# The first block of the hidden gradients read by transposing loads, and two more pairs of weight-gradient stores issued by ScalarE, in a long-convolution plus gated-MLP backward kernel

## The chip, the cores and the metric

The kernel runs on one core of one Trainium2 chip. The metric is device time in microseconds (us), the median of several executions. The engines of the core are TensorE (PE in the profile, with its weight loads shown as PEld), VectorE (DVE), ScalarE (ACT), GpSimd (POOL) and SyncE (SP), which in this kernel issues most of the DMAs. Each engine works through its own queue of instructions in order, and semaphores hold the queues in step.

## The reference, cut to what matters

The program computes a forward pass and all its gradients, in bf16, with S = 2048 rows, D = 512 and F = 1376:

```
xn  = layernorm(q)                              # 2048 x 512
ksh = sum_t shift_k[:, 3-t] * k shifted by t    # four taps
kv  = ksh * v
y   = causal convolution of kv with ssm_k (length 2048, by FFT) + kv * ssm_D
h   = (xn @ Wg) * (xn @ Wu)                     # 2048 x 1376
out = q + xn * y + h @ Wd
outputs: out, and from grad_out the gradients of
         q, k, v, shift_k, ssm_k, ssm_D, Wg, Wu, Wd
```

The part that matters here is the gated MLP. With go = grad_out, its backward pass makes dh = go @ Wd^T, du = dh * (xn @ Wg) and dg = dh * (xn @ Wu), and then the three weight gradients: dWd = h^T @ go, dWg = xn^T @ dg and dWu = xn^T @ du. These three sum over the 2048 rows, so h, dg and du are needed with rows on the partitions, while the forward stage makes them with F on the partitions. Something has to turn them.

## The kernel before

**Tiling.** The 2048 rows lie as 16 rows on each of 128 partitions (R = 16). The first stage works in NCH = 8 chunks of 256 rows. F is cut into NFB = 11 blocks, numbered 0 to 10, ten of 128 and a last one of 96.

**Stage one.** `ffn1(ch)` (L497) makes, for each chunk, a tile `hd` that holds h, dg and du for all eleven blocks, F on the partitions, and stores chunks 0 to 6 to a DRAM scratch `HDD` (L536). Chunk 7 stays in the core. `yb(ch)` (L539) multiplies `hd` by the weights to get the output and the input gradient of the MLP: matmuls into `py` (L548) and `px` (L555); a VectorE addition (L550) adds the loaded rows of q (`xb`, L543) to `py`, and the result `bx` goes to the scratch `BX`. Between these pieces a generator `side` advances the convolution; its last products are cast into `GO` and stored to the scratch `GD` (L619).

**Where the stages meet.** When stage one has no more `ffn1` to do (tag "wa", L897), the pools of two weights are closed, and in their room the core loads `goC` (L902) and `xnC` (L903), go and xn for all rows, 2 MB each. `open_c` (L862) then opens the pools "n" (the turned tiles `nath` and `natd`) and "b" (`g1` and `hb`), and loads blocks 0 and 1 of `HDD` into two `hb` tiles and the first two `g1` tiles out of `GD`.

**How a block is turned.** There are two ways. In the first, block fb is loaded as it lies into `hb` (`load_hb`, L793), and `hid_t(fb, t)` (L846) for t = 0, 1, 2 does 16 TensorE transposes each into a PSUM tile `pt` (L859), which ScalarE copies into `nath` (h) or `natd` (dg and du). Block 0 is turned so between the pieces of `yb(7)`. In the second way, used for the blocks in `TURNED` (6 to 10), `load_t` (L804) issues a transposing DMA (L817) that lands chunks 0 to 6 already turned in a tile `natT`; `last_t` (L824) turns only chunk 7, with 6 TensorE transposes (L829) and one ScalarE copy into `nat7`. `behind` names a DMA that the transposing load of a block must be issued behind.

**The weight gradients.** `dw()` (L1050) goes through the blocks. `down_grad(fb)` makes dWd of the block (`pd`, 16 matmuls, L1038), a cast `od`, and a store. Then come 64 matmuls into `pu` (L1068) for dWg and dWu of the block, and a cast into `og` (L1075). `og` holds two blocks, so after each odd block two stores (L1079, one for dWg and one for dWu) take it to DRAM; there is one `og` buffer. These stores are issued by SP, for blocks 9 and 10 by ScalarE. Halfway through `pu` of block fb, `last_t(fb + 1)` is called if block fb + 1 is a turned one.

**What runs beside it.** Other generators are interleaved with `dw()`: the last transform of y and its gradient (`inv_y`: `pq`, L932, with casts `yC` and `dd`), the gradient of shift_k (`dsk_gram`: `pk`, L1091; its 2 KB result `dskb` is stored at L1107 in pieces of 8 bytes), the gradient of ssm_k (`inv_dk`: `po`, L1003, with casts into `o5t`), and the final elementwise work on VectorE, whose results `o`, `e` and `dk` are stored by SP at L1183. All casts and copies that the helper `act` makes appear under its line, L235.

**What sets the order.** A tile framework puts the instructions in order from priorities, and `issue_after` pins one DMA behind another. The PSUM pool of `pt`, `pu`, `pq`, `po` and `pk` has three buffers, taken in turn. Each DMA issued by SP or ScalarE takes, in program order, the next of eight completion counters. A DMA waits on its issuing engine until the transfer that used its counter before, usually the eighth before it, has landed. While it waits, everything behind it on that engine's queue waits too.

Of the kernel before, what the change touches and what calls it, by code (L numbers as in the profile page):

```python
# [8 lines left out]
BF = mybir.dt.bfloat16  # L9
# [9 lines left out]
D = 512  # L19
F = 1376  # L20
R = 16
P = 128
NC4 = 4
FBLK = [(i * 128, min(128, F - i * 128)) for i in range((F + 127) // 128)]
NFB = len(FBLK)
NCH = 8
# [164 lines left out]
def kernel(  # L191
# [24 lines left out]
    nc = tc.nc  # L216
# [29 lines left out]
    HDD = dram.tile([P, NFB, NCH - 1, 3, 256], BF, name="HDD")  # L246
# [409 lines left out]
    first = ExitStack()  # L656
# [122 lines left out]
    CP = {}  # L779
    nats = {}  # L780
    pend = []

    def load_g1(sg, r0):
        t = CP["b"].tile([P, 2, 4, D], BF, name="g1")
        LG["g"] = nc.sync.dma_start(t[:], GD[sg, :, :, r0:r0 + 4, :])
        return t

    LG = {}

    def load_hb(fb):  # L790
        f0, fw = FBLK[fb]
        t = CP["b"].tile([P, NCH - 1, 3, 256], BF, name="hb")
        nc.sync.dma_start(t[:fw], HDD[:fw, fb])  # L793
        hbs[fb] = t

    hbs = {}

    TURNED = range(NFB - 5, NFB)

    def behind(fb):  # L800
        first = {NFB - 5: lambda: DKS["kb", R - 2], NFB - 3: lambda: LG["gk"], NFB - 2: lambda: LG["bb"], NFB - 1: lambda: LG["og"]}.get(fb)
        return tc.issue_after(first().ins) if first else ExitStack()

    def load_t(fb):  # L804

        f0, fw = FBLK[fb]
        if fb == SPLIT:
            parts = ((0, 5, "n", dict(tag="natd", bufs=2)), (5, NCH - 1, "n", dict(tag="nath")))
        elif fw < P:
            parts = ((0, NCH - 1, "n", dict(tag="natd", bufs=2)),)  # L810
        else:
            parts = ((0, NCH - 1, "b", dict(tag="hb")),)
        nats[fb, 0] = {}
        for a, e, pool, kw in parts:
            t = CP[pool].tile([P, e - a, 3, 2, fw], BF, name="natT", **kw)
            with behind(fb) as _, tc.high_priority(offset=SOON):
                nc.sync.dma_start_transpose(out=t[:].rearrange("s c t h f -> s (c t h) f"),  # L817
                                            in_=HDD[:fw, fb, a:e].rearrange("p c t s -> p (c t s)"))
            for c in range(a, e):
                nats[fb, 0][c] = t[:, c - a]  # L820

    SPLIT = NFB - 3
# [23 lines left out]
    def hid_t(fb, t):  # L846
        if fb in TURNED:
            return
        f0, fw = FBLK[fb]
        hb = hbs.pop(fb) if t == 2 else hbs[fb]  # L850
        if t == 0:
            nats[fb, 0] = CP["n"].tile([P, R, P], BF, name="nath")
        elif t == 1:
            nats[fb, 1] = CP["n"].tile([P, 2, R, P], BF, name="natd", bufs=2)
        dst = nats[fb, 0] if t == 0 else nats[fb, 1][:, t - 1]
        pt = P2("pt", [P, R, P], BF)
        for r in range(R):
            hs = hb[:fw, r // 2, t] if r < R - 2 else hds[1][:fw, fb, t]
            nc.tensor.transpose(pt[:, r, :fw], hs[:, (r % 2) * 128:(r % 2) * 128 + 128], ident[:fw, :fw])  # L859
        act(dst[:, :, :fw], pt[:, :, :fw])  # L860

    def open_c():  # L862
        for _ in side:
            pass
        gpool["es"].close()
        CP["n"] = ctx.enter_context(tc.tile_pool(name="c1n", bufs=1, reuse_waits="tile"))
        CP["b"] = ctx.enter_context(tc.tile_pool(name="c1b", bufs=2, reuse_waits="tile"))
        load_hb(0)
        load_hb(1)
        pend.extend((load_g1(0, 0), load_g1(1, 0)))  # L870

    def main():
        for ch in range(NCH):
            it = ffn1(ch)
            for n, set_here in enumerate(it):
                if ch == 0:
                    tables(n)
                yield set_here
                if n == 1 and 0 < ch < NCH - 1:
                    load_xt(ch + 1)  # L880
                if n == (5 if ch == 1 else 1) and 0 < ch < NCH - 1:
                    while len(WTS) < 2:
                        next(side)
                    yield from yb(ch - 1)
        yield "wa"
        yield from yb(NCH - 2)
        open_c()
        for n, tag in enumerate(yb(NCH - 1)):
            yield tag
            if 2 < n < 6:  # L890
                hid_t(0, n - 3)

    mainit = main()
    acc = -4 * pace[0]
# [1 line left out]
    for tag in mainit:  # L896
        if tag == "wa":  # L897
            wa_es.close()
            c1 = ctx.enter_context(tc.tile_pool(name="c1", bufs=1, reuse_waits="tile"))
            xnC = c1.tile([P, R, D], BF, name="xnC")  # L900
            goC = c1.tile([P, R, D], BF, name="goC")
            nc.sync.dma_start(goC[:], go_n)  # L902
            nc.sync.dma_start(xnC[:], XN[:])  # L903
        if pace[0] is None:

            if tag and tag != "wa":
                next(side, None)
            continue
        if tag != "half":
            acc += pace[0]  # L910
        while acc >= 1 and pace[0]:
            acc -= 1
            next(side, None)
# [28 lines left out]
    DKS = {}  # L942
# [44 lines left out]
        return lambda c, i: ts[c, i // 2][:, i % 2]  # L987

    def inv_dk():
        o5t = c2.tile([P, NC4, P, R], BF, name="o5t", tag="o5k")  # L990
        o5 = out_5.rearrange("(c q) s -> c q s", q=P)
        for rq in range(4):
            gk = gks.pop(0)
            if rq == 2:
                sides[2][1] = 2
            if rq == 0:
                gk_last = load_gk_last()
            for b in range(2):
                po = P2("po", [P, 2, 4, P])
                for h in range(2):  # L1000
                    for i in range(4):
                        for c in range(2):
                            nc.tensor.matmul(po[:, h, i, :], lhsT=(gk_last(c, i) if rq == 3 else gk[:, c, i])[:, cs(2 * b + h)], rhs=TB.IW[:, c, :],  # L1003
                                             start=(c == 0), stop=(c == 1))
                act(o5t[:, 2 * b:2 * b + 2, :, 4 * rq:4 * rq + 4], po[:].rearrange("q h r s -> q h s r"))
                if b == 1 and rq < 2:
                    gks.append(load_gk(2) if rq == 0 else None)
                if rq == 3:
                    for c in (2 * b, 2 * b + 1):
                        nc.scalar.dma_start(o5[c], o5t[:, c].rearrange("q s r -> q (s r)"))  # L1010
                yield
            if rq == 0:
                yield from put_dD(o5t)
# [35 lines left out]

    def dw():  # L1050
        og = None
        load_hb(2)
        for fb, (f0, fw) in enumerate(FBLK):
            last = fb + 1 == NFB
            if not last:
                down_grad(fb)
                yield
                hid_t(fb + 1, 0)
                hid_t(fb + 1, 1)
                yield  # L1060
                yield
            pu = P2("pu", [P, NC4, 2, P])
            if fb % 2 == 0:
                og = c2b.tile([P, 2, NC4, P], BF, name="og1", tag="dd") if last else c2.tile([P, 2, NC4, 2 * P], BF, name="og")
            q0 = (fb % 2) * P
            for c in range(NC4):
                for r in range(R):
                    nc.tensor.matmul(pu[:, c, :, :fw], lhsT=xnC[:, r, cs(c)], rhs=nat_d(fb, r),  # L1068
                                     start=(r == 0), stop=(r == R - 1))
                if c == 1:  # L1070
                    yield
                    if fb + 1 in TURNED:
                        last_t(fb + 1)
                    yield
            act(og[:, :, :, q0:q0 + fw].rearrange("p t c f -> p c t f"), pu[:, :, :, :fw])  # L1075
            if fb % 2 == 1 or last:
                a = f0 - q0
                for t, o in enumerate((out_7, out_8)):
                    LG["og"] = (nc.scalar if fb + 2 >= NFB else nc.sync).dma_start(o[:, a:f0 + fw].rearrange("(c p) f -> p c f", p=128), og[:, t, :, :q0 + fw])  # L1079
            yield  # L1080
            if last:
                down_grad(fb)
                yield
# [76 lines left out]
    KH = []  # L1160

    def load_kh():
        khC = c2.tile([P, R + 3, D], BF, name="khC", tag="o5k")
        nc.gpsimd.memset(khC[0:1, 0:3, :], 0.0)
        with tc.issue_after(LG["g"].ins):
            nc.sync.dma_start(khC[:, 3:3 + R, :], k_n)
            nc.sync.dma_start(khC[1:113, 0:3, :], k_n[0:112, R - 3:R, :])
            nc.sync.dma_start(khC[113:128, 0:3, :], k_n[112:127, R - 3:R, :])
        KH.append(khC)
# [72 lines left out]
```

## Time and profile before

| what | value |
|---|---|
| time, median of three runs | 477.08 us (475.93 to 478.26) |
| time of the profiled execution | 475.32 us |
| its span | 473.5 us |
| granted TensorE clock | 1.00 |
| PE busy | 464.8 us (98%) |
| DVE busy | 339.4 us (72%) |
| ACT busy | 304.6 us (64%) |
| POOL busy | 13.9 us (3%) |
| DMA | 139.86 MB, mean 295 GB/s |

Times in the profile count from the start of the span. The profiled execution lies 1.82 us above its own span and 1.76 us below the median of the runs. A row of a timeline gives the start, the duration, the engine, the line, the operation and its operands, and in brackets how long the engine was idle before it and what released it. "SPq" and "ACTq" are DMAs issued by SyncE and by ScalarE; the duration there is that of the issue, not of the transfer.

### The profile page before, as it was taken

What the parts mean: (1) busy time and instruction counts of PE and PEld (TensorE: products, weight loads), DVE (VectorE), ACT (ScalarE), POOL (GpSimd) and SP (SyncE); (2) the same over time, 40 slices, a digit from 0 to 9 for tenths busy, and PEclk for the clock granted to TensorE, in tenths of its full rate; (3) what the DMA queues carried; (4) which work ended last, traced back from release to release, by engine and by line L of the source; (5) the groups of instructions that cost most, each with busy time, mean ns of one, the idle gap of its engine ahead of it and who ended that gap; (6) DMA issues with size and microseconds to landing.
All of it is one profiled execution on the core that took longest, in us unless ns stands there. A gap on an engine that the chain in (4) does not pass through costs nothing.

```text
span 473.5 us, 10352 instructions
## 1 busy us (share of the span) xinstructions
PE 464.8 (98%) x4263; PEld 310.5 (66%) x4263; DVE 339.4 (72%) x609; ACT 304.6 (64%) x357; POOL 13.9 (3%) x30
## 2 busy tenths in 40 slices
PE   7999999999999999999999999999999999999997
PEld 6877754547638548447537753467776777878887
DVE  7889989989356566777857878113137899799695
ACT  4957777759567678879779975275865664233242
POOL 8000000000000000000000000110000000000000
PEclk9999999999999999999999999999999999999999
DMA  8999999999997958968978369998999999999996
GB/s 264 377 368 383 307 304 328 316 326 321 322 289 262 263 187 256 303 190 263 284 234 277 133 199 367 358 360 289 350 350 365 372 317 333 304 269 313 203 312 199
DMA packets 116917, 139.86 MB, mean 295 GB/s; under 512 B 44776, under 2 KB 90249, under 8 KB 115463
## 3 DMA queue, kind: packets, MB, share of 16 engines
q1 hardware_dynamic: 112598, 135.03, 90.5%
q10 hardware_dynamic: 4272, 4.18, 2.7%
q8 instruction: 33, 0.54, 0.5%
q14 instruction: 14, 0.11, 0.1%
HBM read 65.70 MB, written 63.41 MB: 273 GB/s over the span
## 4 chain that ended last, share of the span: by engine, by line
PE 85%; DMA 8%; DVE 5%; ACT 1%; issue 1%; ACTq 0%
PE pu L1068 16%; PE px L555 16%; PE pgu L512 13%; PE py L548 8%; PE pd L1038 7%; PE pdh L518 6%; PE pt L859 3%; PE pq L932 3%; PE ps L584 3%; PE pg L613 3%; DMA ssk<-in_A_ssm_k_dram 3%; PE pf L370 3%; DMA x_b<-in_A_q_dram 2%; PE pk L1091 2%; PE po L1003 2%; DMA XN<-x_b 1%
## 5 line engine op out<-in xcount | busy, mean ns | idle before, releaser
L555 PE MATMUL px<-WT,hd 128*128 128x512 bf16 (+1 forms) x352 | 81.0, 380 | 0.0
L1068 PEld LDWEIGHTS <-xnC 128*128 128x128 bf16 x704 | 67.1, 98 | 8.2 <-issue 0.4
L555 PEld LDWEIGHTS <-hd 128*128 128x128 bf16 (+1 forms) x352 | 32.8, 98 | 44.4 <-issue 7.7
L235 ACT CAST gu<-pgu 128x1024 bf16<-128x1024 f32 (+1 forms) x48 | 45.4, 945 | 17.3 <-PE pgu L512 16.8
L235 ACT CAST GO<-pg 128x1024 bf16<-128x1024 f32 x48 | 46.2, 1015 | 13.8 <-issue 7.2
L235 ACT CAST SP<-ps 128x1024 bf16<-128x1024 f32 x47 | 45.6, 1026 | 13.7 <-PE ps L584 11.8
L600 DVE TENSOR_TENSOR T<-SP 128x2048 bf16<-128x2048 bf16 x24 | 29.3, 1222 | 34.8 <-ACT SP L235 34.7
L512 PE MATMUL pgu<-xt,Wu 128*128 128x256 bf16 (+1 forms) x352 | 53.1, 273 | 0.7 <-DVE kn L238 0.6
L512 PE MATMUL pgu<-xt,Wg 128*128 128x256 bf16 (+1 forms) x352 | 52.8, 273 | 0.2 <-DMA Wg<-in_B_w_gate_dram 0.2
L518 PE MATMUL pdh<-gt,WdT 128*128 128x256 bf16 (+1 forms) x352 | 46.9, 272 | 0.1
L235 ACT CAST fst<-pf 128x1024 bf16<-128x1024 f32 x44 | 42.7, 1031 | 5.4 <-ACT fst L235 2.1
L1068 PE MATMUL pu<-natd,xnC 128*128 128x256 bf16 x384 | 43.9, 273 | 0.0
L512 PEld LDWEIGHTS <-Wu 128*128 128x128 bf16 (+1 forms) x352 | 33.0, 100 | 15.1 <-issue 10.0
L548 PE MATMUL py<-Wd,hd 128*128 128x512 bf16 (+1 forms) x176 | 41.4, 380 | 0.0
L518 PEld LDWEIGHTS <-WdT 128*128 128x128 bf16 (+1 forms) x352 | 34.9, 100 | 4.8 <-issue 0.2
L512 PEld LDWEIGHTS <-Wg 128*128 128x128 bf16 (+1 forms) x352 | 34.8, 100 | 4.1 <-DMA Wg<-in_B_w_gate_dram 0.5
L1068 PE MATMUL pu<-natT,xnC 128*128 128x256 bf16 (+1 forms) x280 | 32.3, 267 | 0.0
L532 DVE TENSOR_TENSOR hd<-gu 128x512 bf16<-128x512 bf16 (+1 forms) x48 | 19.1, 397 | 17.3 <-ACT gu L235 17.3
L533 DVE TENSOR_TENSOR hd<-gu,dh 128x1024 bf16<-128x1024 bf16 (+1 forms) x48 | 30.8, 642 | 0.8
L235 ACT CAST og<-pu 128x1024 bf16<-128x1024 f32 (+1 forms) x11 | 10.9, 993 | 30.8 <-PE pu L1068 21.4
L548 PEld LDWEIGHTS <-hd 128*128 128x128 bf16 (+1 forms) x176 | 16.5, 98 | 20.8 <-issue 3.1
L600 DVE TENSOR_TENSOR U<-SP 128x2048 bf16<-128x2048 bf16 x24 | 29.2, 1218 | 0.0
(178 smaller groups left out, 685.9 us busy)
## 6 DMA issues: line engine op xcount, KB each, us to landing
HDD<-hd SPq DMA_DIRECT2D x35, 384.0 KB, 4.6
FD<-fst SPq DMA_DIRECT2D x24, 512.0 KB, 5.0
X<-FD SPq DMA_DIRECT2D x24, 512.0 KB, 5.4
GD<-GO SPq DMA_DIRECT2D x24, 512.0 KB, 3.7
g<-GD SPq DMA_DIRECT2D x11, 1024.0 KB, 8.1
hb<-HDD SPq DMA_DIRECT2D x6, 1344.0 KB, 8.4
bb<-BX SPq DMA_DIRECT2D x8, 512.0 KB, 6.8
BX<-bx SPq DMA_DIRECT2D x7, 512.0 KB, 3.9
```

The source lines that it names most:

```text
L235: nc.scalar.copy(o, i)
L370: nc.tensor.matmul(pf[:, c, :], lhsT=TB.W1[:, c, :], rhs=src[:, i, :], start=True, stop=not point)
L512: nc.tensor.matmul(pgu[:w, i, t, :], lhsT=W[:, c, f0:f0 + w], rhs=xt[:, :, c, :], start=(c == 0), stop=(c == NC4 - 1))
L518: nc.tensor.matmul(pdh[:w, i, :], lhsT=WdT[:, c, f0:f0 + w], rhs=gt[:, :, c, :], start=(c == 0), stop=(c == NC4 - 1))
L532: nc.vector.tensor_tensor(hd[:fw, fb0:fb0 + n, 0, :], gu[:fw, :n, 0, :], gu[:fw, :n, 1, :], op=ALU.mult)
L533: nc.vector.tensor_tensor(hd[:fw, fb0:fb0 + n, 1:3, :], gu[:fw, :n], dh[:fw, :n].unsqueeze(2).to_broadcast((fw, n, 2, 256)), op=ALU.mult)
L548: nc.tensor.matmul(py[:], lhsT=hd[:fw, fb, 0, ss], rhs=Wd[:fw, fb, :], start=(fb == 0), stop=(fb == NFB - 1))
L555: nc.tensor.matmul(px[:], lhsT=hd[:fw, fb, t, ss], rhs=W[:fw, fb, :], start=(t == 1 and fb == 0), stop=(t == 2 and fb == NFB - 1))
L584: nc.tensor.matmul(ps[32 * q:32 * q + 32, a, :], lhsT=TB.EF[64 * a:64 * a + 64, 4 * g + q, ri].rearrange("p k j -> p (k j)"), rhs=X[64 * a ...
L600: tt(W[:].rearrange("p c a d -> p c (a d)"), A[:, i:i + 1].rearrange("p c a d -> p c (a d)").to_broadcast((P, 2, 2 * D)), B[:].rearrange(" ...
L1038: nc.tensor.matmul(pd[:fw, :], lhsT=nat_h(fb, r), rhs=goC[:, r, :], start=(r == 0), stop=(r == R - 1))
L1068: nc.tensor.matmul(pu[:, c, :, :fw], lhsT=xnC[:, r, cs(c)], rhs=nat_d(fb, r), start=(r == 0), stop=(r == R - 1))
```

## The change

Block 0 joins the turned blocks. Its transposing load is cut in two: chunks 0 to 4 go into a tile of the pool "n", which is now opened at tag "wa", and SP issues this load ahead of `goC` and `xnC`; chunks 5 and 6 go into a tile that shares its room with `o5t` and `khC` (a new pool "o") and are loaded in `open_c` behind the first `g1`. The plain load of block 0 is gone, and so are its 48 transposes in `yb(7)`; `last_t(0)` runs at the start of `dw()`. `natd` tiles now alternate between two pools instead of taking two buffers of one. The load of block 2 into `hb` comes directly behind that of block 1 and the second `g1`. The stores of `og` of blocks 3 and 7 go from SP to ScalarE. The transposing load of block 10 is pinned behind the load of `bb` instead of behind the stores of `og`.

```diff
-    TURNED = range(NFB - 5, NFB)
+    TURNED = (0, *range(NFB - 5, NFB))
...
-        first = {..., NFB - 1: lambda: LG["og"]}.get(fb)
+        first = {..., NFB - 1: lambda: LG["bb"]}.get(fb)
...
+    def natd(shape, name):
+        i = len(turn) % 2
+        turn.append(i)
+        return CP["nm"[i]].tile(shape, BF, name=name, tag=f"natd{i}")
...
-    def load_t(fb):
+    def load_t(fb, part=None):
         f0, fw = FBLK[fb]
-        if fb == SPLIT:
+        if part is not None:
+            parts = (((0, 5, None, {}),), ((5, NCH - 1, "o", dict(tag="o5k")),))[part]
+        elif fb == SPLIT:
...
-                nc.sync.dma_start_transpose(out=..., in_=...)
+                LG["t"] = nc.sync.dma_start_transpose(out=..., in_=...)
...
     def open_c():
...
-        CP["n"] = ctx.enter_context(tc.tile_pool(name="c1n", bufs=1, reuse_waits="tile"))
+        CP["m"] = ctx.enter_context(tc.tile_pool(name="c1m", bufs=1, reuse_waits="tile"))
         CP["b"] = ctx.enter_context(tc.tile_pool(name="c1b", bufs=2, reuse_waits="tile"))
-        load_hb(0)
+        CP["o"] = ctx.enter_context(tc.tile_pool(name="c1o", bufs=1, reuse_waits="tile"))
+        pend.append(load_g1(0, 0))
+        load_t(0, 1)
         load_hb(1)
-        pend.extend((load_g1(0, 0), load_g1(1, 0)))
+        pend.append(load_g1(1, 0))
...
         yield from yb(NCH - 2)
         open_c()
-        for n, tag in enumerate(yb(NCH - 1)):
-            yield tag
-            if 2 < n < 6:
-                hid_t(0, n - 3)
+        yield from yb(NCH - 1)
...
+            CP["n"] = ctx.enter_context(tc.tile_pool(name="c1n", bufs=1, reuse_waits="tile"))
+            load_t(0, 0)
             nc.sync.dma_start(goC[:], go_n)
             nc.sync.dma_start(xnC[:], XN[:])
...
     def dw():
         og = None
-        load_hb(2)
+        with tc.issue_after(LG["t"].ins):
+            load_hb(2)
+        last_t(0)
...
-                    LG["og"] = (nc.scalar if fb + 2 >= NFB else nc.sync).dma_start(...)
+                    LG["og"] = (nc.scalar if fb in (3, NFB - 4, NFB - 2, NFB - 1) else nc.sync).dma_start(...)
```

More of the change, by code (lines that the diff above doesn't have):

```diff
@@ L796 @@
     hbs = {}
-    TURNED = range(NFB - 5, NFB)
+    TURNED = (0, *range(NFB - 5, NFB))
     def behind(fb):
-        first = {NFB - 5: lambda: DKS["kb", R - 2], NFB - 3: lambda: LG["gk"], NFB - 2: lambda: LG["bb"], NFB - 1: lambda: LG["og"]}.get(fb)
+        first = {NFB - 5: lambda: DKS["kb", R - 2], NFB - 3: lambda: LG["gk"], NFB - 2: lambda: LG["bb"], NFB - 1: lambda: LG["bb"]}.get(fb)
         return tc.issue_after(first().ins) if first else ExitStack()
-    def load_t(fb):
+    turn = []
+    def natd(shape, name):
[3 more added lines that the diff above has]
+    def load_t(fb, part=None):
         f0, fw = FBLK[fb]
-        if fb == SPLIT:
-            parts = ((0, 5, "n", dict(tag="natd", bufs=2)), (5, NCH - 1, "n", dict(tag="nath")))
+        if part is not None:
+            parts = (((0, 5, None, {}),), ((5, NCH - 1, "o", dict(tag="o5k")),))[part]
+        elif fb == SPLIT:
+            parts = ((0, 5, None, {}), (5, NCH - 1, "n", dict(tag="nath")))
         elif fw < P:
-            parts = ((0, NCH - 1, "n", dict(tag="natd", bufs=2)),)
+            parts = ((0, NCH - 1, None, {}),)
         else:
             parts = ((0, NCH - 1, "b", dict(tag="hb")),)
-        nats[fb, 0] = {}
+        if not part:
+            nats[fb, 0] = {}
         for a, e, pool, kw in parts:
-            t = CP[pool].tile([P, e - a, 3, 2, fw], BF, name="natT", **kw)
+            shape = [P, e - a, 3, 2, fw]
+            t = CP[pool].tile(shape, BF, name="natT", **kw) if pool else natd(shape, "natT")
             with behind(fb) as _, tc.high_priority(offset=SOON):
-                nc.sync.dma_start_transpose(out=t[:].rearrange("s c t h f -> s (c t h) f"),
-                                            in_=HDD[:fw, fb, a:e].rearrange("p c t s -> p (c t s)"))
+                LG["t"] = nc.sync.dma_start_transpose(out=t[:].rearrange("s c t h f -> s (c t h) f"),
+                                                      in_=HDD[:fw, fb, a:e].rearrange("p c t s -> p (c t s)"))
             for c in range(a, e):
@@ L853, in hid_t @@
         elif t == 1:
-            nats[fb, 1] = CP["n"].tile([P, 2, R, P], BF, name="natd", bufs=2)
+            nats[fb, 1] = natd([P, 2, R, P], "natd")
         dst = nats[fb, 0] if t == 0 else nats[fb, 1][:, t - 1]
@@ L989, in inv_dk @@
     def inv_dk():
-        o5t = c2.tile([P, NC4, P, R], BF, name="o5t", tag="o5k")
+        o5t = CP["o"].tile([P, NC4, P, R], BF, name="o5t", tag="o5k")
         o5 = out_5.rearrange("(c q) s -> c q s", q=P)
@@ L1078, in dw @@
                 for t, o in enumerate((out_7, out_8)):
-                    LG["og"] = (nc.scalar if fb + 2 >= NFB else nc.sync).dma_start(o[:, a:f0 + fw].rearrange("(c p) f -> p c f", p=128), og[:, t, :, :q0 + fw])
+                    LG["og"] = (nc.scalar if fb in (3, NFB - 4, NFB - 2, NFB - 1) else nc.sync).dma_start(o[:, a:f0 + fw].rearrange("(c p) f -> p c f", p=128), og[:, t, :, :q0 + fw])
             yield
@@ L1162, in load_kh @@
     def load_kh():
-        khC = c2.tile([P, R + 3, D], BF, name="khC", tag="o5k")
+        khC = CP["o"].tile([P, R + 3, D], BF, name="khC", tag="o5k")
         nc.gpsimd.memset(khC[0:1, 0:3, :], 0.0)
```

## The prediction, made before the changed kernel had run

> **What bounds the kernel now.** I began with the page's head, its busy times and the shares of the chain that ended last.
>
> ```profile
> span 473.5 us, 10352 instructions
> ...
> PE 464.8 (98%) x4263; PEld 310.5 (66%) x4263; DVE 339.4 (72%) x609; ACT 304.6 (64%) x357; POOL 13.9 (3%) x30
> ...
> PE 85%; DMA 8%; DVE 5%; ACT 1%; issue 1%; ACTq 0%
> ```
>
> PE is busy for 98% of the span, so only two things move the time much: PE work added or removed, and stalls of PE. The change touches two places. For the first, where block 0 is turned, the chain that ended last, in order of time:
>
> ```profile
> 305.60 0.87 PE px L555 x4
> 306.47 0.89 PE pt L859 x16
> 307.36 1.51 PE px L555 x7
> 308.87 0.90 PE pt L859 x16
> 309.77 2.38 PE px L555 x11
> 312.15 0.90 PE pt L859 x16
> 313.04 3.45 PE pd L1038 x16
> ```
>
> The three batches of transposes stand between matmuls with no gap: what they cost is PE time on the path. For the second place, where block 7's `og` is stored, SP's timeline:
>
> ```profile
> 428.47 9.52 SPq L817 DMA_TRANSPOSE natT<-HDD  x1
> 438.08 0.53 SPq L1045 DMA_DIRECT2D out_dram<-od  x1
> 438.66 0.42 SPq L1107 DMA_DIRECT2D out_dram<-dskb  x1
> ...
> 442.38 0.97 SPq L1079 DMA_DIRECT2D out_dram<-og  x2
> 445.71 6.70 SPq L817 DMA_TRANSPOSE natT<-HDD  x1
> ```
>
> and ScalarE's, where the last three lines show what a ScalarE store does when the transfer that had its counter is still out:
>
> ```profile
> 435.65 1.01 ACT L235 CAST og<-pu 128x1024 bf16<-128x1024 f32 x1 [2.69 <-PE pu L1068]
> 436.55 1.02 ACT L235 CAST o5t<-po 128x1024 bf16<-128x1024 f32 x1
> ...
> 461.59 1.01 ACT L235 CAST og<-pu 128x1024 bf16<-128x1024 f32 x1 [2.19 <-PE pu L1068]
> 464.88 1.94 ACTq L1079 DMA_DIRECT2D out_dram<-og  x2
> 466.87 0.80 ACT L235 CAST og<-pu 128x768 bf16<-128x768 f32 x1 [4.27 <-PE pu L1068]
> ```
>
> Block 9's cast ends at 462.60, yet its stores issue at 464.88 and the next cast starts only behind them: ScalarE stood. Last, PE's row for the chunk-7 transposes of block 9, and a line of SP's waits:
>
> ```profile
> 444.18 0.50 PE L829 MATMUL pt<-ident,hd 128*128 128x128 bf16 x6
> ```
>
> ```profile
> SPq L817 <- DMA out_dram<-dskb: 2.3, 1, 2.3
> ```
>
> The `dskb` store, issued at 438.66, lands only at 445.66 (7.0 us for 2 KB in 8-byte pieces, behind block 9's transposing load); whoever has its counter next waits for it. Before, that was the transposing load of block 10 on SP, with no harm to PE.
>
> **The change part by part.** All sums are on the clock of the profiled execution (475.32 us, span 473.5), which lies 1.76 below the median of 477.08; I add that back at the end.
>
> *Transposes.* Removed from PE: 0.89 + 0.90 + 0.90 = 2.69 us. Added: six transposes for chunk 7, by the step between PE rows at 444.18 and 444.51, 0.33 us. Net −2.35. ScalarE loses three copies (1.86 each at 307.40, 309.81, 313.18) and gains one of 0.80; no PE instruction waited there, so nothing either way. Bounds: 0 if the same stretch becomes a stall, −2.35 if none does; I take −2.35, since the loads come in time:
>
> *Loads.* The plain load of block 0 (1.34 MB) goes; 0.98 MB and 0.39 MB of transposing loads come. The first stands on SP ahead of `goC`, `xnC`, a `GD` store and `xb`. Up to now the DMA engines are empty from 274 to 278 (share 0.00) and full from 282 to 294 (0.99, 382 GB/s). `xb`, issued at 290.74, landed at 295.4; in the changed kernel it must be in and the 0.69 us addition done before PE's second `py` of `yb(7)` at 303.06, which takes the same PSUM buffer. The load pushes it by 0.98 MB at 382 GB/s (2.6 us) or, if what counts is SP's issue time, by 6.2 us (7.65 for block 8's two parts less 1.39 for the smaller); a 0.5 MB `GD` store now ahead adds 1.4. So `xb` lands between 299.4 and 303.0: a stall of 0 to 0.6, and I take 0. The other first users have more room: the small part (chunks 5 and 6) lands about 307 and `pd` needs it near 312; `g1` about 311 against 314; block 1 about 314 against 315.7; block 2 about 320 against 330. Later transposing loads are far ahead: block 9's landed at 441.6 for PE at 448.9.
>
> *One tile fewer.* `nat7` of block 0 sits in one of the two `dd` buffers until `pu(0)` ends, so the second `dd` cast must wait for VectorE's two products of the first (until about 326.8 instead of 325.4). The next cast it could delay is `og` at 328.76: 0.
>
> *Stores of block 3.* They wait for a `g1` load and a part of `khC`, both landed by 375.4, while the cast of block 3 ends at 379.49. ScalarE pays two issues of about 0.45 us; ScalarE is 64% busy and no PE row waits for it there. 0; bounds 0 to 0.9.
>
> *Stores of block 7.* By the order of DMAs and the eight counters, the first must wait for the `od` store of SP 438.08 (landing 442.1), the second for `dskb` (445.66). Queued behind them on ScalarE: the cast `o5t` that ran at 436.55, then `od`, `o5t`, `nat7`. PE's six transposes for block 9 take the PSUM buffer which that first `o5t` cast must empty. So they can start at 445.66 + 0.45 (second issue) + 1.02 (cast) + about 0.1 = 447.2 instead of 444.18, a stall of 3.1 us. Both ends move together if SP's chain moves with PE: block 7's transposing load (398.05) waited 7.2 us for PE, and the `og` stores of 412.31 follow a cast driven by PE, so everything up to `dskb` should be 2.35 earlier, like PE itself. Bounds: 0 (no stand, or `dskb` in before 440.2 on the new clock) and 5.4 (SP's chain keeps its old times, 3.1 + 2.35). I take 3.1, nearest to the rows.
>
> *The tail.* Behind it nothing is gained back: PE follows on without idle. `og` of block 8 is cast when the late stores have landed; `pu` of block 9 has 1.07 us of room (cast end 452.18, `pu` 453.25), which a landing of 2.6 us, the median of ScalarE's `og` stores, leaves whole. VectorE's last `dk`, today 0.35 us in the way of the last `od` store, is earlier with SP, so −0.3.
>
> Sum: −2.35 + 3.1 − 0.3 = +0.45: 475.8 on the profiled clock, 477.5 against the median.
>
> [...]
>
> **The rivals.** *A: the cover holds.* ScalarE doesn't stand long enough to stop PE, because `dskb` lands early or the stores' counters are free. For it: only 2 KB are written, and PE has never yet waited for a ScalarE store. Against: the order of transfers gives exactly this counter, and ScalarE did stand at 462.60 to 464.88. It gives −2.35 to −2.65: 474.6. [...]
>
> *B: slower, SP's chain stays where it is.* One mechanism, at one place: `dskb` lands on the old clock. The chain ahead of it is 7.65 and 9.52 us of issue for transposing loads; if these are bound by the engines that move them (share 1.41 from 434 to 440) and not by PE's release, PE arrives 2.35 us early and waits 5.4. Price: −2.35 + 5.4 − 0.3 = +2.8, 479.8. It decides from a landing of `dskb` at about 445.3 on the new clock. The stores of ScalarE in the same engines could push it there too. Against: SP was released by PE at 398.05.
>
> *C: the front is late as well.* `xb` or `goC` comes after the issue of 6.2 us plus more traffic, PE loses about 1 us at 303: with the main case 478.5. For it: SP's slowest bound above is 0.6 already; against: 4 us of empty DMA engines ahead of it.
>
> **How the numbers follow.** Main case (gain eaten by the ScalarE stand, 476.7 to 478.5 with 0 to 1 for C): 0.53, with C in it. A: 0.22. B: 0.25. The bound that a measurement of this kernel can tell is 0.5%, 2.4 us: faster means below 474.7, slower above 479.5. A's 474.4 to 474.7 lies at or under the one and B's 479.9 at or over the other, so the chances are nearly the cases' own: faster 0.21, same 0.54, slower 0.25. Range: from A's lower end, 474.4, to B's with 0.4 for a late `xb`, 480.2. The main case's own range is 476.7 to 478.7.
>
> **What would show it.** In the changed profile: `px` of `yb(7)` in one piece with no `pt`, and `pd` of block 0 about 2.35 us earlier than 313.04 (else C, at the row of the second `py`); on ScalarE a gap between `og` of block 7 and its two stores, and the first `o5t` only behind the second; a PE idle of about 3 us ahead of the six transposes of block 9; the landing of `dskb` on the new clock, 443.3 for the main case, 445.3 or later for B, before 440.5 for A. The prediction is wrong if PE shows no idle there, if the idle is over 5, or if a new PE wait appears elsewhere, at `pu` of block 9 or `po`, for which no row of before gives a reason.

## The result, and the profile after

The changed kernel is slower: 480.62 us median of nine runs (478.24 to 482.92), against 476.69 us of the kernel before in as many (475.63 to 478.26). The ratio is 1.0084, with a 95% interval of 1.006 to 1.0109: 2.9 to 5.2 us more. (The ratios in this document leave out executions that took over 1.5% more than the fastest of their kernel, and so are not the quotient of the two medians beside them, which are over all executions.) The forecast was 477.5, in a range from 474.4 to 480.2, with 0.25 for slower by over 0.5%. The median lies 0.4 us above the range.

The profiled execution of the changed kernel took 480.96 us, with a span of 479.2, 5.7 more than the span of before. Its page begins:

```profile
span 479.2 us, 10219 instructions
...
PE 462.3 (96%) x4181; PEld 310.2 (65%) x4221; DVE 339.0 (71%) x609; ACT 299.9 (63%) x355; POOL 14.0 (3%) x30
...
PE 79%; DMA 12%; DVE 6%; issue 1%; ACT 1%; ACTq 0%; SPq 0%; DVEq 0%
```

PE's busy time is 2.5 us lower (this trace has 4181 matmuls for 4221 weight loads, so some matmul records are missing from it), and the span is longer. PE's share of the chain that ended last fell from 85% to 79%, and DMA's rose from 8% to 12%. The chain itself, in order of time:

```profile
305.97 1.30 PE px L555 x6
307.27 0.05 issue
307.32 3.41 PE px L555 x15
310.73 0.34 PE pt L840 x6
311.07 3.45 PE pd L1050 x16
...
365.83 15.41 DMA hb<-HDD
381.25 0.05 issue
381.30 1.96 PE pt L870 x32
...
439.46 5.52 DMA out_dram<-od
444.98 0.02 issue
445.00 0.02 ACTq L1093
...
446.27 1.02 ACT o5t L235
447.29 0.04 issue
447.33 0.80 PE pt L840 x6
448.13 5.89 PE pu L1082 x32
```

Three things are to be seen. The `px` matmuls run on with no transposes between them, and six transposes stand ahead of `pd`. At 365.83 a load is on the path that was not there before: block 5's plain load, which reaches PE at 381.25. And from 439.46 the chain leaves PE altogether: a store of `od`, ScalarE's two stores of `og`, the `o5t` cast, and only then PE's six transposes for block 9. Here are SP's and ScalarE's timelines of that place, and PE's row; SP's first row is block 7's load, the second block 9's.

```profile
396.73 10.31 SPq L828 DMA_TRANSPOSE natT<-HDD  x1
...
429.69 9.68 SPq L828 DMA_TRANSPOSE natT<-HDD  x1
439.46 0.52 SPq L1057 DMA_DIRECT2D out_dram<-od  x1
440.04 0.42 SPq L1121 DMA_DIRECT2D out_dram<-dskb  x1
...
444.80 7.95 SPq L828 DMA_TRANSPOSE natT<-HDD  x1
```

```profile
434.32 1.01 ACT L235 CAST og<-pu 128x1024 bf16<-128x1024 f32 x1 [2.69 <-PE pu L1082]
445.06 1.17 ACTq L1093 DMA_DIRECT2D out_dram<-og  x2
446.27 1.01 ACT L235 CAST o5t<-po 128x1024 bf16<-128x1024 f32 x1 [10.94 <-issue]
```

```profile
447.33 0.80 PE L840 MATMUL pt<-ident,hd 128*128 128x128 bf16 x6 [4.31 <-ACT o5t L235]
447.93 3.19 PE L1082 MATMUL pu<-natT,xnC 128*128 128x256 bf16 x14
```

ScalarE stood from 435.33, the end of block 7's cast, to 445.06, and PE was idle for 4.31 us. The counters can be read in this trace: its 322 DMAs of SP and ScalarE take eight semaphores in turn, 40 or 41 on each, and ScalarE's two stores here have those of `od` and `dskb`, which were full at 444.98 and 445.16; the stores issued at 445.06 and 445.49. And behind the idle PE's rows are longer for the same work: six transposes in 0.80 us, where the row of before says 0.50, and 14 `pu` matmuls in 3.19 where the others say 1.69. The windows of the changed kernel say why; the columns are the busy times of PE, PEld, DVE, ACT and POOL, the granted clock of PE, the DMA share and the GB/s:

```profile
443.00:447.00 4.00, 0.02 (x1) 0.00 (x0) 3.44 (x7) 0.73 (x1) 0.00 (x0) 0.89 0.83 196
...
448.00:450.00 2.00, 2.00 (x12) 1.40 (x10) 1.79 (x4) 1.39 (x2) 0.00 (x0) 0.50 0.98 177
450.00:452.00 2.00, 2.00 (x12) 1.34 (x10) 1.93 (x4) 0.00 (x0) 0.00 (x0) 0.50 1.24 247
452.00:454.00 2.00, 2.00 (x17) 1.63 (x16) 1.97 (x6) 0.00 (x0) 0.00 (x0) 0.77 1.24 258
```

The granted clock is a half from about 446 to 453. It was 1.00 in these windows before, and the mean over the span is 0.993 or 0.996 in all nine executions of the changed kernel.

From these rows the 5.7 us can be followed. PE's positions, changed less before: +0.38 at 271 us, before any changed instruction (the `pdh` rows at 271.38 and 271.00); −1.98 at `pd` of block 0 (310.90 and 312.88), so the turning gave 2.36; −1.32 at block 5's transposes (381.30 and 382.62), so 0.66 was lost at the late load; +3.15 at block 9's six transposes (447.33 and 444.18), so the stand took 4.47; +5.85 at the `po` matmuls behind block 8's `pu` (453.86 and 448.01), so the half clock took 2.70; then level to the end, where the tail gives 0.15 back.

### The profile page after: what moved, and what is told of

Read it like the earlier page. It is cut to its first block, busy times and chain, and to the rows that moved or that the text cites. A ratio compares the mean times of both kernels' runs of the same rounds, so it can differ in the third digit from the quotient of the medians.

```text
span 479.2 us, 10219 instructions
## 1 busy us (share of the span) xinstructions
PE 462.3 (96%) x4181; PEld 310.2 (65%) x4221; DVE 339.0 (71%) x609; ACT 299.9 (63%) x355; POOL 14.0 (3%) x30
## 4 chain that ended last, share of the span: by engine, by line
PE 79%; DMA 12%; DVE 6%; issue 1%; ACT 1%; ACTq 0%; SPq 0%; DVEq 0%
PE px L555 15%; PE pu L1082 14%; PE pgu L512 13%; PE py L548 7%; PE pd L1050 6%; PE pdh L518 6%; DMA hb<-HDD 3%; PE ps L584 3%; PE pf L370 3%; PE pg L613 3%; DMA ssk<-in_A_ssm_k_dram 2%; PE pq L944 2%; PE pt L870 2%; DMA x_b<-in_A_q_dram 2%; PE pk L1105 2%; PE po L1015 1%
## 5 line engine op out<-in xcount | busy, mean ns | idle before, releaser
L555 PE MATMUL px<-WT,hd 128*128 128x512 bf16 (+1 forms) x340 | 78.5, 379 | 1.6 <-issue 1.4
L1082 PEld LDWEIGHTS <-xnC 128*128 128x128 bf16 x704 | 68.4, 100 | 9.4 <-issue 0.4
L1082 PE MATMUL pu<-natT,xnC 128*128 128x256 bf16 (+1 forms) x336 | 41.4, 277 | 0.0
L548 PE MATMUL py<-Wd,hd 128*128 128x512 bf16 (+1 forms) x167 | 40.2, 379 | 0.8 <-issue 0.5
L1082 PE MATMUL pu<-natd,xnC 128*128 128x256 bf16 x320 | 36.6, 273 | 0.0
```

What stands on the lines that cost most here:

```text
L548: nc.tensor.matmul(py[:], lhsT=hd[:fw, fb, 0, ss], rhs=Wd[:fw, fb, :], start=(fb == 0), stop=(fb == NFB - 1))
L555: nc.tensor.matmul(px[:], lhsT=hd[:fw, fb, t, ss], rhs=W[:fw, fb, :], start=(t == 1 and fb == 0), stop=(t == 2 and fb == NFB - 1))
```

## The experiments

**The loads alone.** Block 0 turned by transposing loads as in the change; all stores and the pin of block 10's load as before.

```diff
-  (nc.scalar if fb in (3, NFB - 4, NFB - 2, NFB - 1) else nc.sync)
+  (nc.scalar if fb + 2 >= NFB else nc.sync)
-  NFB - 1: lambda: LG["bb"]
+  NFB - 1: lambda: LG["og"]
```

> The changed kernel's loads without its moves of stores: block 0 turned by transposing loads; all og stores and the pin of block 10's load as in the kernel before. Theory: first pd of block 0 about 2.35 us earlier than before, of which about 0.65 is lost at block 5's plain load, which lands at the same clock time as before; 1.7 us under the kernel before, 475.0. Rival (the transfers are shared out so that nothing is gained): the time of before within 0.5 us. Rival (nothing is late next): 2.35 under, 474.3.

Measured: 474.55 us against 476.18, ratio 0.997 (0.9946 to 0.9993). Its span is 472.4. `pd` of block 0 starts 39.53 us after the `pdh` row near 271, against 41.88 before: 2.35 gained, to the hundredth what was forecast for the turning. In this execution block 5's load was in time, as the second rival had it. So the loads are a small gain by themselves, and the whole loss belongs to the moved stores and the moved pin.

**Block 3's stores.** As the loads alone, with block 3's stores on ScalarE:

```diff
-  (nc.scalar if fb + 2 >= NFB else nc.sync)
+  (nc.scalar if fb in (3, NFB - 2, NFB - 1) else nc.sync)
```

> The loads-only kernel with block 3's two stores of og issued by ScalarE; block 7's stay on SyncE and block 10's load stays pinned behind them. Theory (block 3's stores are harmless): as loads only, 474.6, within 1 us, no idle of TensorE in the second half. Rival (they cost the bound of 0.9 us or more): above 475.5.

Measured: 475.82 against 476.69, ratio 0.996 (0.993 to 0.9991). The median lies above the 475.5 that the rival named, but the kernel before ran 0.5 us longer here than beside the loads alone. Against its own kernel before, the ratio is no worse than theirs (0.997), so no cost of these stores is clear of the noise. In the profile PE waited once, which the theory did not have: 1.16 us ahead of block 9's `pu` (at 452.25, for block 8's cast of `og`). No half clock followed: the mean over the span is 1.000. One of the ten executions took 480.33 us, at a mean clock of 0.996; it has no profile.

**Block 7's stores back on SP.** The changed kernel, its pin kept:

```diff
-  fb in (3, NFB - 4, NFB - 2, NFB - 1)
+  fb in (3, NFB - 2, NFB - 1)
```

> The changed kernel, only with block 7's two stores of og back on SyncE (block 3's stay on ScalarE). Theory (the loss is ScalarE standing at block 7's stores, then TensorE at half clock): no idle of TensorE ahead of the six transposes of block 9, granted clock 1.00 throughout, the gain of 2.35 us of transposes less about 0.65 us for the late load of block 5: 1.7 us under the kernel before, about 475.0. Rival (the loss comes from the later transposing loads on SyncE): the idle stays, time at or above the kernel before. Rival (block 3's stores cost as well): between 475.5 and 477.

Measured: 478.42 against 476.18, ratio 1.0022 (1.0001 to 1.0043). The idle ahead of block 9's transposes is gone, as expected, but the kernel is not 1.7 us under the kernel before. Its waits of PE begin with

```profile
PE pu L1082 <- ACT og L235: 3.2, 1, 3.2
```

and SP's timeline shows what came in its place:

```profile
444.11 5.96 SPq L828 DMA_TRANSPOSE natT<-HDD  x1
450.17 1.07 SPq L1093 DMA_DIRECT2D out_dram<-og  x2
```

With the pin behind `bb`, block 10's transposing load goes ahead of block 7's stores on SP and holds them for its 5.96 us of issue. The one `og` buffer comes free late, block 8's cast is late (453.93 instead of 451.17), and PE waits for that cast's PSUM buffer at block 9's `pu`. Behind the idle of 3.22 us the clock fell to 0.50 again, from 455 to 458. I had seen the pin only as a matter of order and given it no price.

**The pin alone.** The kernel before, with nothing changed but

```diff
-  NFB - 1: lambda: LG["og"]
+  NFB - 1: lambda: LG["bb"]
```

> The kernel before with only block 10's load pinned behind bb, so that it goes ahead of block 7's og stores on SyncE. Theory (from the run with block 7's stores back on SyncE, where the load of 6 us held them up): the stores issue near 449 instead of 442.4, land near 453.5, block 8's cast of og ends near 454.6 and block 9's pu starts there instead of 453.25: idle of 1 to 3 us, 477.5 to 479. Rival (the pin cost only under the new loads): as before.

Measured: 482.21 against 476.69, ratio 1.0092 (1.0058 to 1.0127), about as much as the whole change costs (1.0084), and over the top of the expectation. That had 1 to 3 us of idle, where the profile shows 3.4, and it had left out the clock (0.992 or 0.996 in all ten executions). The wait is the same one:

```profile
PE pu L1068 <- ACT og L235: 3.4, 1, 3.4
```

So the pin is not free unless block 7's stores leave SP with it. The two parts of the change belong together.

**Block 7's stores on ScalarE without the loads.** The kernel before, with block 7's stores on ScalarE and the pin behind `bb`:

```diff
-  (nc.scalar if fb + 2 >= NFB else nc.sync)
+  (nc.scalar if fb in (NFB - 4, NFB - 2, NFB - 1) else nc.sync)
-  NFB - 1: lambda: LG["og"]
+  NFB - 1: lambda: LG["bb"]
```

> The kernel before with block 7's stores on ScalarE and block 10's load pinned behind bb; block 0 turned by TensorE. The two stores take the counters of block 9's transposing load (landed at 441.6) and of block 7's od store (442.1), so ScalarE is free at about 442.6, the o5t cast ends at 443.6 and TensorE needs it at 444.18. Theory (it is the shift of 3 us between TensorE, earlier, and SyncE, later, under the new loads that makes the stand bite): no idle there, time of before within 1 us, unless the stores, now beside block 10's load, land late for the next og cast. Rival (ScalarE's stand bites whatever the loads do): idle of 3 us, 479 or more.

Measured: 476.80 against 476.69, ratio 0.9994 (0.9964 to 1.0024): no change. ScalarE's and PE's rows:

```profile
443.33 0.99 ACTq L1079 DMA_DIRECT2D out_dram<-og  x2
444.36 1.01 ACT L235 CAST o5t<-po 128x1024 bf16<-128x1024 f32 x1 [6.81 <-DMA out_dram<-od]
```

```profile
445.43 0.49 PE L829 MATMUL pt<-ident,hd 128*128 128x128 bf16 x6 [0.19 <-ACT o5t L235]
```

ScalarE stands here too, for 5.8 us from 437.55, but PE came later and found the cast done but for 0.19 us. So the stand is not new with the loads; it bites with them. The run differs from the changed kernel in block 3's stores as well, and so in which transfers the two stores wait for, but this matters little: here the first store was released as block 9's load landed (430.47 + 12.78 = 443.25), and in the changed kernel `od`, for which the first store waited, landed 0.2 us behind block 9's load.

**The same without block 3's stores.** The changed kernel, with only block 3's stores back on SP:

```diff
-  fb in (3, NFB - 4, NFB - 2, NFB - 1)
+  fb in (NFB - 4, NFB - 2, NFB - 1)
```

> The changed kernel with block 3's stores back on SyncE: loads, block 7's stores on ScalarE, block 10's load pinned behind bb. Its second store takes the counter of the od store of block 7 and not that of dskb. Theory (ScalarE stands for SyncE's late od store and TensorE with it): idle of about 4 us ahead of block 9's transposes, the clock at 0.50 for some 6 us behind it, 480 to 481. Rival (dskb's counter is the cause): no idle over 2 us, below 478.

Measured: 478.95 against 476.69, ratio 0.9994 (0.995 to 1.0037). The ratio hides what happened, for the ten executions fall into two groups: 473.04, 473.58 and 475.77 us at a mean clock of 0.999 or 1.000, where the rival had them, and seven from 478.23 to 482.67 at 0.993 or 0.996, around the theory's 480 to 481. Both groups are one kernel with the same counters, so the counter of the second store does not decide between them. The profile is of the first group, its span 471.8:

```profile
427.37 9.47 SPq L828 DMA_TRANSPOSE natT<-HDD  x1
```

```profile
442.65 0.50 PE L840 MATMUL pt<-ident,hd 128*128 128x128 bf16 x6 [0.24 <-ACT o5t L235]
```

In this execution SP issued block 9's load at 427.37, 2.32 us earlier than in the changed kernel's profile, and the idle was 0.24 us. The first of ScalarE's stores waited for block 9's load, which landed at 438.87. The kernel stands on an edge: some 2 us in SP's chain go with the difference between 473 and 479. No profile of the second group was taken.

**Block 7's stores behind the copy PE waits for.** The changed kernel, but ScalarE issues these two stores only behind the copy of block 9's six transposes (and `og` is taken from its pool just ahead of the cast):

```diff
+                    with tc.issue_after(LG["n7"].ins):
+                        for put in held:
+                            put()
...
-                    LG["og"] = ....dma_start(...)
+                    if fb == NFB - 4:
+                        held.append(put)
+                    else:
+                        put()
```

> The changed kernel, with block 7's two stores issued by ScalarE only behind the copy of block 9's transposes, so that nothing TensorE needs for these stands behind them; their counters are now those of a dk store and of the load of bb. Theory (ScalarE's stand ahead of the o5t cast is what stopped TensorE): no idle ahead of block 9's transposes; what is late next is the og buffer, since the stores now run beside block 10's load and land about 453 to 455, so block 9's pu waits 2 to 4 us for block 8's cast, 476.5 to 479. Rival (the idle came from the loads): the idle ahead of block 9's transposes stays, 480 or more.

Measured: 478.50 against 476.12, ratio 1.0037 (1.0006 to 1.0067), and PE's waits begin with

```profile
PE pu L1081 <- ACT og L235: 4.3, 1, 4.3
```

There is no idle ahead of block 9's transposes. So it was ScalarE's stand in front of the `o5t` cast that stopped PE there. Late next is the `og` buffer, as expected: the stores issue at 448.33, beside block 10's load, and block 8's cast waits until 456.14.

**The stand for ScalarE's reasons alone.** The kernel before, with n copies of 128 columns in front of the `o5t` cast that empties the PSUM buffer of block 9's transposes; no DMA and no store is moved. They copy a part of what the cast then writes.

```diff
+                if rq == 1 and b == 1:
+                    for _ in range(n):
+                        act(o5t[:, 2, :, 4], po[:, 0, 0, :])
                 act(o5t[:, 2 * b:2 * b + 2, :, 4 * rq:4 * rq + 4], po...)
```

> The kernel before, with 22 more copies of 128 columns on ScalarE in front of the o5t cast whose PSUM buffer the six transposes of block 9 take (each copies a part of what that cast writes anyway). At some 0.33 us each, ScalarE reaches that cast later and TensorE idles about 2 us ahead of those transposes; no DMA is moved. [...] Rival (any stall brings the half clock): clock 0.996, 3 to 4 us over.

> As the run with 22 copies, with 26: an idle of about 3.3 us. [...] Rival (the clock fell because of the DMA traffic at that place): 1.00 in all, 3 us over.

> As the run with 22 copies, with 31: an idle of about 5 us. Theory: all executions below 0.997, the six transposes at 0.8 us and the 32 pu matmuls behind them near 5.9 us instead of 3.5, 7 to 8.5 us over the kernel before. Rival (DMA traffic): clock 1.00, 5 us over.

Measured, with two executions each: 485.26, 486.35 and 490.61 against 476.12, ratios 1.0194, 1.0217 and 1.0307. As a ladder of idles they failed: each copy took about 0.74 us instead of 0.33, and since the scheduler mixed other casts in, PE's idle ahead of these transposes was 6.0 us in all three. For the clock they answer. With 22 copies, PE's row:

```profile
452.76 0.80 PE L829 MATMUL pt<-ident,hd 128*128 128x128 bf16 x6 [6.05 <-ACT o5t L235]
```

The idle was made by ScalarE and by no transfer, and PE's work is again at half pace behind it; but DMAs ran there as well. With 31 copies PE idled a second time, and there the DMA engines were empty (the last two columns are the DMA share and the GB/s):

```profile
462.20 1.87 PE L1003 MATMUL po<-IW,g 128*128 128x128 bf16 x16 [3.78 <-ACT nat L235]
```

```profile
458.00:460.00 2.00, 0.42 (x4) 0.23 (x3) 1.97 (x6) 1.94 (x3) 0.00 (x0) 1.00 0.53 201
460.00:462.00 2.00, 0.00 (x0) 0.00 (x0) 1.97 (x5) 1.94 (x4) 0.00 (x0) 0.61 0.00 0
462.00:464.00 2.00, 1.80 (x17) 1.80 (x17) 1.86 (x3) 1.97 (x4) 0.00 (x0) 0.50 0.38 139
464.00:466.00 2.00, 2.00 (x7) 0.60 (x5) 1.93 (x3) 1.64 (x2) 0.00 (x0) 0.50 0.00 0
```

The clock fell to a half in a stretch in which nothing was transferred. So the half clock came here in an idle of PE, of 3.78 us, and without DMA traffic.

**Two that missed their aim.** The kernel before with block 7's stores on ScalarE and the pin left on `og`:

```diff
-  (nc.scalar if fb + 2 >= NFB else nc.sync)
+  (nc.scalar if fb in (NFB - 4, NFB - 2, NFB - 1) else nc.sync)
```

> The kernel before, only with block 7's two stores of og issued by ScalarE; block 0 is turned by TensorE as before. Theory: ScalarE stands until the dskb store has landed (445.7), TensorE starts block 9's six transposes near 447.2 instead of 444.18, an idle of about 3 us; if that leaves the clock at 1.00 the time is 2.8 us over the kernel before (479.5), if the clock falls to a half behind it, 5.5 over (482.2). Rival (the stand needs the new loads): no idle, time as before.

Measured: 482.24 against 476.18, ratio 1.0128 (1.0064 to 1.0191), but for another reason. The pin no longer held block 10's load, which is SP's, once the store it names was ScalarE's: SP issued it at 416.65 together with block 8's two parts (13.13 us for the three), everything behind it on SP came some 5 us late, and PE was not stopped at block 9's transposes at all (444.34, no idle). In this profile the time was lost at the end; the three other executions, at 481.19 to 486.39, read mean clocks of 0.991 to 0.994 and have no profile. The run tells nothing of the stand. It shows that here a pin held only while the load and the store it names were on one queue. And the first try at idle copies:

```diff
+            if fb == NFB - 4:
+                for _ in range(44):
+                    act(idle[:], ident[:])
```

> The kernel before with 44 idle copies of 128x128 on ScalarE between block 7's cast of og and the next cast, no DMA and no store moved. It makes TensorE wait at block 9's six transposes for a reason of ScalarE alone. A copy should take between 0.16 and 0.28 us (128 columns at the 1.7 us of a 2048-column copy are 0.11, and the smallest copy of the profile, 128x4, takes 0.20), so ScalarE is held 7 to 12 us and TensorE idles 0.5 to 5.7 us. [...]

Measured: one execution, 482.92. The copies depend on nothing, and the scheduler put them between 318 and 350 us, not behind block 7's cast. It says nothing on the stand. For the clock it gives one point: PE's longest idle was 1.7 us, for a `yC` cast, and no half clock shows in the mean over the span, 0.999.

## Why the prediction was wrong

**Transposes: right.** Forecast −2.35; 2.36 in the changed kernel, 2.35 and 2.34 in the two runs with the loads and no stand.

**Loads: right at the front, with one cover missed.** `xb` was added from 301.75 to 302.44, inside the forecast bounds and ahead of PE's need. But I followed the new first users only, and not block 5's plain load: issued only 0.5 us earlier than before (365.83 for 366.34), it landed at about the same time (381.2 for 381.5, 15.4 and 15.2 us behind the issue), so PE, earlier by 2, met it. It cost 0.66 us in the changed profile, 0.4 and 1.1 in two of the others with the new loads and nothing in the other three.

**Block 3's stores: right**, at nothing that is clear of the noise.

**Block 7's stores: the step that failed is "everything up to `dskb` should be 2.35 earlier, like PE itself".** It was not. The first link did move: block 7's load was issued at 396.73 for 398.05, earlier by the 1.32 us that PE then was. But its issue took 10.31 us, and the lead was gone. SP's rows of this load, from the kernel before and from the run without block 3's stores (the changed kernel's stands above):

```profile
398.05 7.88 SPq L817 DMA_TRANSPOSE natT<-HDD  x1
```

```profile
396.12 7.58 SPq L828 DMA_TRANSPOSE natT<-HDD  x1
```

Behind it SP kept its old pace: 7.68 and 9.68 us of issue for blocks 8 and 9, where 7.65 and 9.52 stood. So block 9's load was issued 1.22 us later than before. It also took 15.1 us to land where it had taken 13.1, and `od` landed right behind it, at 444.98 instead of 442.1. That landing, and not `dskb`'s as I had it, released the first of ScalarE's stores. The second issued at 445.49, behind `dskb`, which had landed at 445.16, about the landing of 445.3 from which the slower rival was to decide. PE's transposes began at 447.33, about where I had put them on the old clock (447.2), but PE was there 1.32 us earlier: the stand took 4.47 us where I had 3.1 and the rival 5.4.

The other profiles agree. Counted from PE's `pdh` row near 271, SP issued block 9's load on average at 157.9 in the three profiles with the old turning and this order of loads (the kernel before and the two runs made from it with the pin behind `bb`), and at 158.0 in the six with the new one, though PE was 1.3 to 2.35 us earlier in these; among themselves the executions differ by up to 3.3. `od` landed 3.8 to 4.0 us behind its issue in the three, and 5.5 to 6.1 in five of the six. The sixth is the run without block 3's stores: there block 7's load took 7.58 us, `od` landed in 2.2, and PE hardly stood. So the slower rival had the effect right, at 0.25, and the reason in part: the issue times that it named did stay, but the lead was lost at the load ahead of them, whose issue became longer, and more was lost at the landing.

**A term that was in no sum: the clock behind the idle.** I priced a stall of PE by its length. It also cost 2.70 us at half clock. The kernel before could not show it, since it has no idle of PE that long in this stage; its longest wait of PE anywhere is 1.4 us. In the rows of the runs 3.22, 4.31 and 6.05 us of idle brought 0.50, and 1.16 and 1.7 did not. Length alone does not tell when the clock falls: with 31 copies it fell 4.2 us into PE's first idle (446.0 to 452.0) and 2.0 us into the second (458.4 to 462.2). From the mean clocks of that run's windows it was a half from 450.2 to 457.0 and from 460.4 to 467.2, so the steps are 6.8, 3.4 and 6.8 us apart. What sets these times was not shown. No idle in these rows ended between 1.7 and 3.22 us.

With both corrections, −2.36 + 0.66 + 4.47 + 2.70 − 0.15 and the 0.38 from ahead of the change make the 5.7 of the profiles, where I had 0.45. Of the 5.2 between, the clock is the largest part with 2.7, and the longer stand has 1.4. The medians differ by 3.9, since the executions vary by some us and the profiled one of before, 475.32, lay below all nine.

**The tail**: forecast −0.3, measured −0.15.

**The rival that the cover holds** fell: ScalarE stood for 9.73 us, and PE for 4.31 behind it. The stand is in the queue of the engine that issues: with the stores moved behind the copy that PE needs, the idle at that place went. As transfers the stores cost nothing that was seen: without the loads, block 7's on ScalarE gave 0.9994.

**Not settled:** what makes block 7's load take 7.6 or 10 us to issue, and why block 9's landed later, and so which executions of the kernel on the edge stall. The 14 profiles give a hint. Block 7's load took 7.6 to 8.0 us to issue where SP had finished issuing the two loads of `g` ahead of it at least 3.3 us before, and 8.8 to 10.7 where that was 2.7 us or less. With PE earlier, this distance is shorter (2.64 us in the changed profile, 3.30 before). No run moved it alone, so that it is the cause is not shown.

The loads alone (0.997) and with block 3's stores on ScalarE (0.996) are faster than the kernel before, by little, with intervals that end just under 1; the two do not differ by more than their intervals.

## What to carry to other kernels

Work taken off the busiest engine moved that engine here (PE, by 1.3 to 2.35 us), and not the queue that feeds and drains it (SP's issue of block 9's load, 157.9 and 158.0 us behind PE's `pdh` row): check each transfer that has less slack than the gain, and ask for each wait whether both its ends really move. Before a store is given to another engine, look at which earlier transfer it must wait for, and at what stands behind it in that engine's queue; the wait that was idle time on SyncE (2.3 us) became TensorE's (4.31). A stall of TensorE of some us is to be priced with the slow stretch that may follow it: 3.22 us brought one here, 1.7 did not, and behind the stand of 4.47 it cost 2.70, another 60%.

## What the runs showed that I had not expected

The half clock is visible in the mean of an execution: the profiled ones with no long idle ahead of the tail have 0.998 to 1.000, those with one 0.992 to 0.996, and the one with two 0.986. A change of order of one load, with no work added, cost 4.4 us of 476 (ratio 1.0092). And a copy of 128 columns on ScalarE took 0.30 us where it was independent of the one before, and about 0.74 us where each wrote the place of the last. The slower ones also read PSUM and write with a stride, and the runs don't separate these.
